# Six more key blocks on VectorE, feed-forward and output rows interleaved, and TensorE's waits divided, in a fused attention and gated feed-forward kernel

## The chip, the cores and the metric

One core of a Trainium2 chip runs the whole program. The metric is the device time of one execution in microseconds (us); the kernel before takes 685.96 us, the median of three runs from 685.57 to 686.65.

## The reference

The input x has 2048 rows of 512 values in bf16. Its layer norm xn feeds an attention with 32 heads of width 16 and a gated feed-forward of width 1792, and the result is the sum of both and x:

```python
xn = layernorm(x)                                  # 2048 x 512
q, k, v = split(xn @ wqkv)                         # 32 heads, 16 wide
p = softmax(q @ k.T * 16 ** -0.5)                  # per head, 2048 x 2048
A = merge(p @ v) @ wo
gate, up = xn @ W_gate, xn @ W_up                  # 2048 x 1792
B = (where(gate > 0, gate, 0) * up) @ W_down
out = x + A + B
```

The softmax has 32 x 2048 x 2048 exponentials, and these set the shape of the kernel.

## The kernel before, in words

**Tiling.** Queries come in four quarters of 512 (`c4`), heads in four groups of eight (`gg`), each in an even and an odd half (`ee`). That makes 32 *table blocks*, counted from 0 in the order of the work, and each of them goes over 16 *key blocks* of 128 keys for four heads.

**Two ways to exponentiate.** A key block on ScalarE is two *units*. A unit (loop at L1353) is two score groups on TensorE (`score`, L1289) into a PSUM buffer of two banks, of which there are two, and one exp over 128 x 1024 on ScalarE (L1365) into a ring of sixteen buffers. After both units come two groups that multiply with v (`pv_stream`, L1244). A key block on VectorE (`quad`, L1312) is four score groups, four evictions (L1320) that turn a score into an integer whose bits read as a bf16 exponential, two shifted copies of that (a *pattern* each), and six v groups, as the three approximations are summed. The string `QUAD_AT` (L67) says by table block and key block which key blocks go this way: a dot stays on ScalarE, and in the digit each bit says that one pattern is made on GpSimd, in two pieces (L1335), and otherwise on VectorE (L1339). With mask 2 the first pattern is VectorE's and the second GpSimd's. GpSimd's pieces wait by semaphore for VectorE's last pattern. 153 key blocks are on VectorE, and the other 359 are 718 units.

**TensorE's groups.** Nearly all matmuls are 64 x 32 tiles with 512 columns, issued as *groups* of four that fill one half of the array (64 rows); two groups, one in each half, run at the same time. Weights are loaded ahead in each half.

**Background jobs.** Projections of q, k and v, the feed-forward and the output rows run between the scores, through four further PSUM banks. A *feed-forward tile* (`glu`, L992) is two chains of eight groups, each with an eviction on VectorE (L1016, L1020), and gives an h tile of 128 x 512. An *output row tile* (`out_rows`, L1034) is 18 products, 36 groups: fourteen h tiles with `W_down` and four head groups with `wo`; one VectorE addition of x (L1069) and a store end it. `mm_chain` (L816) makes the groups. All of a row's groups name the same `reads`: all h tiles, all of `W_down`, `wo` and the attention results, so the first of them waits for all. After the feed-forward tiles of a quarter come its four output rows together (L1114); h has 20 slots. The rows of the last quarter come at the end and hold back part of their sum for a tail (`normalise_last`, L1136).

**What sets the order.** The program isn't scheduled when it is built: the string `PLAN` lists all operations in the order of a planner made beforehand, and the slots of their buffers (`run`, L324). Each engine takes its operations strictly in that order. `emit` (L380) turns dependencies into semaphores. `play` (L475) issues, before an operation, one wait per semaphore that it needs; where there are several, all but one become instructions of their own on the engine's queue (recorded at L483). DMAs go through SP's queue, and a stream of DMAs shares one semaphore.

Of the kernel before, what the change touches and what calls it, by code (L numbers as in the profile page):

```python
# [16 lines left out]
S = 2048  # L17
# [26 lines left out]
ROW_AT = 20  # L44
XBANKS = (0, 1, 2, 3)
# [32 lines left out]
    "2...3..3..2..3..",  # L78
    "2...3..3..0..3..",
    "2...3..3..2..3..",  # L80
# [5 lines left out]
    "3...3..3..2..3..",  # L86
    "2...2..3..0..3..",
    "2...3..3..2..3..",
    "2...3..3..2..3..",
# [4 lines left out]
    "2...3..3..2..3..",  # L94
    "2...3..3..0..3..",
    "2...3..3..2..3..",
# [145 lines left out]
class Op:  # L242
    __slots__ = ("eng", "dur", "fn", "deps", "order", "prio", "acq", "name", "idx", "start", "end",
                 "done", "left", "users", "signal", "sem", "val", "waits", "stream", "lat", "seq", "cseq", "hb", "after", "mode", "half", "bank", "urgent", "slack", "port",
                 "load", "wsrc", "wkey", "wwaits", "pair")


def matmul_loaded(e, out, w, x, start, stop, at):

    return e.add_instruction(mybir.InstMatmult(  # L250
        name=e.bass.get_next_instruction_name(), engine=mybir.EngineType.PE, ins=[e.lower_ap(x), e.lower_ap(w)], outs=[e.lower_ap(out)],
        start_tensor_calc=start, stop_tensor_calc=stop, tile_size=(64, 32), tile_position=at, ldweights=False))
# [1165 lines left out]
```

## Time and profile before

| | |
|---|---|
| median of the runs, us | 685.96 |
| the profiled execution: span from first to last instruction, us | 684.2 |
| its time outside the span | not given by the profile |
| granted TensorE clock, mean | 0.999 |
| exps on ScalarE (L1365) | 718 |
| score evictions on VectorE (L1320) | 612 |
| patterns on VectorE (L1339), pieces on GpSimd (L1335) | 83, 446 |
| 64 x 32 matmuls in the exp phase (10.9 to 674.2 us) | 21,959 |

Each engine's busy time is the union of its instructions. TensorE (PE), its weight loads (PEld) and ScalarE (ACT) overlap the end of one instruction with the next, so a short wait between two needn't show as idle time; starts in the timeline show it. A row of the timeline joins equal instructions without idle time between them: start, length, engine, line, operation and count, and in brackets the idle time before and what ended it. A row of the windows view has for each engine the busy time and the number of instructions in that window.

### The profile page before, as it was taken

Reading aid. Unit: us, or ns where it says so; the run is one execution under the profiler, and the core shown is the slowest. Engines: PE = TensorE matmul, PEld = TensorE weight load, DVE = VectorE, ACT = ScalarE, POOL = GpSimd, SP = SyncE. Lnnn points to the kernel's source line nnn. Section 1 sums busy time; section 2 is a strip of 40 time slices with the busy share of each in tenths; the row PEclk is TensorE's granted clock in tenths of the full one; section 3 lists DMA queues with packets and bytes.
Section 4 is the critical chain, followed back from the end, with each engine's and each line's share of the span. In section 5 each row is a group of like instructions: output and inputs, shape, how many; then the busy total and the mean of one; then the engine's idle time right before and its main releaser. Section 6 shows DMA issues by size and latency. Waiting matters only on the chain.

```text
span 684.2 us, 45020 instructions
## 1 busy us (share of the span) xinstructions
PE 675.6 (99%) x22262; PEld 345.9 (51%) x19654; DVE 598.5 (87%) x1012; ACT 666.8 (97%) x730; POOL 499.8 (73%) x507
## 2 busy tenths in 40 slices
PE   8999999999999999999999999999999999999998
PEld 4455454545555554554444455554554455555543
DVE  9958899999989787999999788889998887988875
ACT  6999999999999999999999999999999999999994
POOL 3323768678688778887587886888878868787792
PEclk9999999999999999999999999999999999999999
DMA  7430220113122021212101022120202012131011
GB/s 216 57 75 12 58 77 27 33 55 91 56 65 66 5 77 34 69 41 63 35 23 31 10 78 63 38 69 5 56 27 61 25 53 62 44 86 42 22 36 54
DMA packets 55940, 35.86 MB, mean 52 GB/s; under 512 B 19336, under 2 KB 51784, under 8 KB 55752
## 3 DMA queue, kind: packets, MB, share of 16 engines
q1 hardware_dynamic: 55464, 32.71, 17.4%
q8 instruction: 164, 2.69, 1.6%
q10 hardware_dynamic: 288, 0.26, 0.1%
q14 instruction: 24, 0.20, 0.1%
HBM read 26.35 MB, written 2.35 MB: 42 GB/s over the span
## 4 chain that ended last, share of the span: by engine, by line
PE 75%; ACT 18%; DVE 5%; issue 1%; DMA 0%; POOL 0%; ACTq 0%
PE ps L250 75%; ACT ring L1365 18%; DVE stats L726 1%; DVE qd L1320 1%; DVE xn_sb L739 1%; DVE v_aug L876 0%; DMA x_sb<-in_A_x_dram 0%; DVE qT L952 0%; DVE mv L727 0%; ACT xn_sb L1164 0%; DVE qd L1339 0%; DVE xnT L780 0%; POOL rstd L721 0%; DVE xnT L1075 0%; DVE kT L869 0%
## 5 line engine op out<-in xcount | busy, mean ns | idle before, releaser
L1365 ACT ACTIVATE ring<-ps 128x1024 bf16<-128x1024 f32 x718 | 660.4, 1141 | 2.9 <-PE ps L250 2.5
L1335 POOL TENSOR_TENSOR qd<-qd,ints 128x512 int32<-128x512 int32 x446 | 450.5, 1041 | 143.8 <-DVE qd L1339 73.2
L250 PE MATMUL ps<-qT,kT 64*32 64x512 bf16 x8192 | 448.7, 374 | 1.3 <-DVE qd L1320 0.4
L1320 DVE TENSOR_SCALAR qd<-ps 128x512 int16<-128x512 f32 x612 | 396.7, 685 | 51.9 <-PE ps L250 49.0
L250 PE MATMUL ps<-qd,v_aug 64*32 64x512 bf16 x3672 | 263.0, 375 | 1.1 <-issue 0.9
L250 PE MATMUL ps<-ring,v_aug 64*32 64x512 bf16 x2872 | 236.5, 374 | 0.1
L1300 PEld LDWEIGHTS <-kT 64*32 64x32 bf16 x7584 | 151.1, 92 | 126.6 <-issue 32.6
L1272 PEld LDWEIGHTS <-v_aug 64*32 64x32 bf16 x4544 | 108.7, 91 | 75.6 <-issue 20.4
L250 PE MATMUL ps<-xnT,wgs 64*32 64x512 bf16 x1792 | 137.6, 374 | 0.0
L250 PE MATMUL ps<-xnT,wus 64*32 64x512 bf16 x1792 | 136.4, 374 | 0.0
L250 PE MATMUL ps<-Wd,hT 64*32 64x512 bf16 x768 | 59.0, 375 | 0.0
L810 PEld LDWEIGHTS <-wgs 64*32 64x32 bf16 x1792 | 43.1, 91 | 31.5 <-issue 7.4
L810 PEld LDWEIGHTS <-wus 64*32 64x32 bf16 x1792 | 43.2, 91 | 29.8 <-issue 7.6
L1339 DVE TENSOR_SCALAR qd<-qd 128x2048 int16<-128x2048 int16 x83 | 56.1, 690 | 2.3 <-PE ps L250 2.2
L810 PEld LDWEIGHTS <-hT 64*32 64x32 bf16 x1792 | 40.2, 92 | 28.2 <-issue 4.2
L250 PE MATMUL ps<-Wv,hT 64*32 64x512 bf16 x512 | 45.7, 375 | 0.0
L250 PE MATMUL ps<-Wk,hT 64*32 64x512 bf16 x512 | 42.8, 375 | 0.4 <-DVE qd L1320 0.3
L1020 DVE SCALAR_TENSOR_TENSOR hT<-ps,up_sb 128x512 bf16<-128x512 f32 x56 | 38.4, 685 | 4.6 <-PE ps L250 4.2
L1016 DVE COPY up_sb<-ps 128x512 f32<-128x512 f32 x56 | 38.4, 685 | 3.1 <-PE ps L250 2.5
L250 PE MATMUL ps<-Wo_p,x_sb 64*32 64x512 bf16 x480 | 40.2, 374 | 0.6 <-issue 0.5
L250 PE MATMUL ps<-xnT,Wq 64*32 64x512 bf16 x480 | 36.2, 375 | 0.0
L250 PE MATMUL ps<-xnT,Wk 64*32 64x512 bf16 x480 | 35.0, 374 | 0.3 <-DVE xnT L780 0.3
(70 smaller groups left out, 263.8 us busy)
## 6 DMA issues: line engine op xcount, KB each, us to landing
rb<-rec_scr SPq DMA_DIRECT2D x31, 256.0 KB
wus<-in_B_W_up_dram SPq DMA_DIRECT2D x38, 128.0 KB, 2.8
wgs<-in_B_W_gate_dram SPq DMA_DIRECT2D x38, 128.0 KB, 3.3
xr_sb<-in_A_x_dram SPq DMA_DIRECT2D x16, 128.0 KB, 2.6
qT<-qf SPq DMA_DIRECT2D x120, 16.0 KB, 2.6
out_dram<-xn_sb SPq DMA_DIRECT2D x14, 128.0 KB, 2.0
x_sb<-in_A_x_dram SPq DMA_DIRECT2D x8, 128.0 KB, 2.8
x_sb<-oT SPq DMA_DIRECT2D x60, 16.0 KB, 2.5
```

The costliest lines, as they stand in the source:

```text
L250: return e.add_instruction(mybir.InstMatmult(name=e.bass.get_next_instruction_name(), engine=mybir.EngineType.PE, ins=[e.lower_ap(x), e.lo ...
L726: G.op("DVE", 580, lambda e, m=m: e.bn_stats(stats[:, m, :], xs(m)), reads=[t_xm[m]], writes=[t_st], prio=pr, order=last_xn if m == 4 else ())
L739: G.op("DVE", 320, lambda e, m=m, t=t_n: e.tensor_scalar(xn_sb[:, t.slot, :], xs(m), mv[:, m, 0:1], rstd[:, m:m + 1], op0=ALU.subtract, op ...
L810: e.ldweights(w()[rows, 32 * j:32 * j + 32], tile_position=(rows.start, 32 * j))
L1016: G.op("DVE", 603, lambda e: e.tensor_copy(up_sb[:, tup.slot, :], bank_of(tu)), reads=[tu], writes=[tup], prio=-590)
L1020: G.op("DVE", 603, lambda e: e.scalar_tensor_tensor(out=hT[:, th.slot, :], in0=bank_of(tg), scalar=0.0, in1=up_sb[:, tup.slot, :], op0=ALU ...
L1272: e.ldweights(vs(j), tile_position=(64 * half, 32 * j))
L1300: e.ldweights(ks(m), tile_position=(64 * half, 32 * m))
L1320: G.op("DVE", 601, lambda e, j=j, tx=tx: e.tensor_scalar(qd[:, tq.slot, 512 * j:512 * j + 512], ps[:, BANK[tx.slot], :], IBIAS[3], 0.0, op ...
L1335: G.op("POOL", POOL_NS / POOL_PIECES + 60, lambda e, x=x, n=n, c=slice(i * m, i * m + m): e.tensor_tensor(x().bitcast(I32)[:, c], raw().bi ...
L1339: G.op("DVE", 600, lambda e, n=n, x=x: e.tensor_scalar(x(), raw(), float(SHIFTS[n + 1]), None, op0=ALU.add), reads=[ti, tq], writes=[t], p ...
L1365: exp_ops[u] = G.op("ACT", 904, lambda e, tr=tr, k0=k0: e.activation(ring[:, tr.slot, :, :], ps[:, 4 * k0:4 * k0 + 2, :], ACTF.Exp, scale= ...
```

## The change

Four things change together, and the order of the plan with them: `PLAN_OPS` goes from 8248 to 8302, and `PLAN` is another string (left out here).

1. Six strings of `QUAD_AT`, those of table blocks 10, 12, 18, 21, 26 and 28, get a sixth key block on VectorE, all with mask 2. It is 159 key blocks on VectorE then, and 706 units.
2. The output rows of a quarter are held back (`behind`) and dealt out between the feed-forward tiles of the next quarter, one after each `ROW_STEP` of them: none, one, two and two. As the h tiles live longer for that, twelve more h slots lie in `xnT`, in the quarters whose projections are done (`h_of`, and the guards at the end).
3. With `each=True`, a product in an output row reads only its own h tile and its own slice of the weights (`only`), so its groups wait part by part.
4. In `emit`, where a TensorE operation has several waits, all but the latest are moved, where possible, to one of the eight operations before it: to its second to fourth matmul, at most three. The producer must stand more than 20 places of the plan before that carrier, or 70 if it is a DMA.

Besides, the packing DMAs of attention results use four semaphores each in place of two.

```diff
+ROW_STEP = (0, 1, 2, 2)
...
-    "2...3..3..2..3..",
+    "2.2.3..3..2..3..",
...
-    "3...3..3..2..3..",
+    "3.2.3..3..2..3..",
...
+CARRIED = []
 def matmul_loaded(e, out, w, x, start, stop, at):
+    if at[1] and CARRIED:
+        e.wait_ge(*CARRIED.pop(0))
...
+    CARRY_BACK, CARRY_AGE, CARRY_AGE_DMA = 8, 20, 70
...
+        for i, o in enumerate(q):
+            best = {}
+            for d in o.waits:
+                s, v = d.sem
+                if id(s) not in best or best[id(s)][1] < v:
+                    best[id(s)] = (s, v, d)
+            for s, v, d in sorted(best.values(), key=lambda b: b[2].start)[:-1]:
+                for p in q[max(0, i - self.CARRY_BACK):i][::-1]:
+                    if p.mode != "half" or p.start <= d.start + (self.CARRY_AGE_DMA if d.eng == "SP" else self.CARRY_AGE):
+                        break
+                    if len(carried.get(p, ())) < 3:
+                        carried.setdefault(p, []).append((s, v))
+                        moved_off.setdefault(o, set()).add(id(s))
+                        break
...
-                wait(o.waits)
+                wait(o.waits, moved_off.get(o, ()))
+                CARRIED[:] = carried.get(o, ())
...
-        P_h = Pool("h", NHS)
+        P_h = Pool("h", NHS + 12)
...
-                    G.op("PE", 216, fn, reads=reads, joins=[tile],
+                    need = reads[i] if each else reads
+                    G.op("PE", 216, fn, reads=need, joins=[tile],
...
+        def h_of(t):
+            if t.slot < NHS:
+                return hT[:, t.slot, :]
+            a, dt = divmod(t.slot - NHS, 4)
+            return xnT[:, dt, 512 * a:512 * a + 512]
...
-            th = t_h[(c4, ft)] = Tile("h", P_h)
+            th = t_h[(c4, ft)] = Tile("h", P_h, list(range(NHS)) + [NHS + 4 * a + dt for a in range(c4) for dt in range(4)
+                                                               if c4 < NB - 1 or a == 2 or dt in TAIL_ACT])
...
-            pairs, reads = [], [t_wo]
+            pairs, reads = [], []
             if first:
-                reads += [t_h[(c4, ft)] for ft in range(FT)] + [t_wd]
                 for ft in range(FT):
+                    reads.append([t_h[(c4, ft)], only(t_wd, ft)])
...
-                reads.append(to)
+                reads.append([to, only(t_wo, g)])
...
-            mm_chain(t, pairs, reads, pr, slots=slots, sub=sub)
+            mm_chain(t, pairs, reads, pr, slots=slots, sub=sub, each=True)
...
-            seq += rows
+            step = ROW_STEP[c4]
+            for n, row in enumerate(behind):
+                seq += tiles[n * step:n * step + step] + [row]
+            seq += tiles[len(behind) * step:]
+            behind = rows
+        seq += behind
...
-                    stream=("pk", j, (n // 2) % 2), name="pk")
+                    stream=("pk", j, (n // 2) % NGG), name="pk")
...
+        for a in range(3):
+            guard = Tile("xnT")
+            guard.r.extend(o for o in t_xnT[a].w + t_xnT[a].r if o not in resids)
+            P_h.cur[NHS + 4 * a:NHS + 4 * a + 4] = [guard] * 4
```

More of the change, by code (lines that the diff above doesn't have):

```diff
@@ L367, in run @@
                 port[o.eng] = o
-            o.seq = len(self.queue[o.eng])
+            o.seq, o.start = len(self.queue[o.eng]), i
             self.queue[o.eng].append(o)
@@ L814, in bass_parallel_sum__mha_block__glu_gated_reglu__prompt_kernel, with mm_chain @@
         chains = [0]
-        def mm_chain(tile, pairs, reads, prio, sub=0, slots=None, mode="half", weights=None, flags=None):
+        def mm_chain(tile, pairs, reads, prio, sub=0, slots=None, mode="half", weights=None, flags=None, each=False):
             n = len(pairs)
@@ L1032, in resid, with only @@
             return xnT[:, i, 0:1024].bitcast(FP32)
+        def only(t, n):
+            part = Tile()
+            part.w.append(t.w[n])
+            return part
         def out_rows(c4, i, gs, first, last, slots=None, pr=0.0, tile=None, sub=0):
```

234 lines of the change are left out of this document (122 added, 112 removed).

## The prediction

> **What bounds the kernel now.** First the page's totals, the chain, and the costliest groups.
>
> ```profile
> span 684.2 us, 45020 instructions
> ...
> PE 675.6 (99%) x22262; PEld 345.9 (51%) x19654; DVE 598.5 (87%) x1012; ACT 666.8 (97%) x730; POOL 499.8 (73%) x507
> ...
> PE 75%; ACT 18%; DVE 5%; issue 1%; DMA 0%; POOL 0%; ACTq 0%
> ...
> L1365 ACT ACTIVATE ring<-ps 128x1024 bf16<-128x1024 f32 x718 | 660.4, 1141 | 2.9 <-PE ps L250 2.5
> L1335 POOL TENSOR_TENSOR qd<-qd,ints 128x512 int32<-128x512 int32 x446 | 450.5, 1041 | 143.8 <-DVE qd L1339 73.2
> L250 PE MATMUL ps<-qT,kT 64*32 64x512 bf16 x8192 | 448.7, 374 | 1.3 <-DVE qd L1320 0.4
> L1320 DVE TENSOR_SCALAR qd<-ps 128x512 int16<-128x512 f32 x612 | 396.7, 685 | 51.9 <-PE ps L250 49.0
> ...
> L1339 DVE TENSOR_SCALAR qd<-qd 128x2048 int16<-128x2048 int16 x83 | 56.1, 690 | 2.3 <-PE ps L250 2.2
> ```
>
> TensorE at 99% and ScalarE at 97% cannot both be believed: both pipeline, so busy time hides short waits. The starts decide. Two answers of the timeline of ScalarE alone: the whole run, then a stretch without a wait.
>
> ```profile
> 10.91 2.87 ACT L1365 ACTIVATE ring<-ps 128x1024 bf16<-128x1024 f32 x3
> 14.10 146.19 ACT L1365 ACTIVATE ring<-ps 128x1024 bf16<-128x1024 f32 x159 [0.32 <-PE ps L250]
> 160.47 2.85 ACT L1365 ACTIVATE ring<-ps 128x1024 bf16<-128x1024 f32 x3 [0.17 <-PE ps L250]
> 163.63 22.10 ACT L1365 ACTIVATE ring<-ps 128x1024 bf16<-128x1024 f32 x24 [0.31 <-PE ps L250]
> 186.10 38.83 ACT L1365 ACTIVATE ring<-ps 128x1024 bf16<-128x1024 f32 x42 [0.37 <-PE ps L250]
> 225.36 182.36 ACT L1365 ACTIVATE ring<-ps 128x1024 bf16<-128x1024 f32 x198 [0.42 <-PE ps L250]
> 408.64 265.61 ACT L1365 ACTIVATE ring<-ps 128x1024 bf16<-128x1024 f32 x289 [0.92 <-PE ps L250]
> 680.25 0.60 ACT L1164 ACTIVATE xn_sb<-ps 128x512 bf16<-128x512 f32 x1 [6.00 <-PE ps L250]
> ```
>
> ```profile
> 126.28 19.35 ACT L1365 ACTIVATE ring<-ps 128x1024 bf16<-128x1024 f32 x21
> ...
> 144.36 2.19 ACT L1365 ACTIVATE ring<-ps 128x1024 bf16<-128x1024 f32 x2
> ```
>
> From the first exp of that stretch to the 21st are 20 intervals in 144.36 - 126.28 = 18.08 us: **0.904 us** from exp to exp when nothing is late, although one exp lasts 1.14 us. The exps run from 10.91 to 408.64 + 265.61 = 674.25 us, 663.3 us. 717 intervals at 0.904 us are 648.2, the last exp adds 1.1, and 14.0 us are left: **lateness**, 20 ns per exp. Every visible one of these waits ends on a TensorE score. Before the first exp stand 10.9 us, after the last 10.0 us. So ScalarE sets the pace for 98% of the exp phase, and TensorE's lateness for the other 2%.
>
> TensorE has room in spite of its 99%:
>
> ```profile
> 10.90:674.20 663.30, 659.61 (x21959) 338.40 (x19374) 585.20 (x969) 660.39 (x719) 493.62 (x492) 1.00 0.18 50
> ```
>
> ```profile
> 407.72 0.39 PE L250 MATMUL ps<-qd,v_aug 64*32 64x512 bf16 x4
> 407.74 0.38 PE L250 MATMUL ps<-Wd,hT 64*32 64x512 bf16 x4
> ...
> 407.94 0.39 PE L250 MATMUL ps<-qd,v_aug 64*32 64x512 bf16 x4
> ...
> 407.96 0.38 PE L250 MATMUL ps<-Wd,hT 64*32 64x512 bf16 x4
> ```
>
> Eight matmuls, four in each half of the array, start every 0.21 to 0.22 us. The exp phase has 21,959 of them: 2,745 such rounds, at 0.215 us 590 us of 663, or 89%. The full clock is granted (1.00).
>
> **The change, part by part.** *Six more blocks on VectorE.* A key block on ScalarE is two exps; one on VectorE is four evictions (L1320), one pattern on VectorE (L1339), two pieces on GpSimd (L1335; all six have mask 2), ten groups of four matmuls in place of six. Twelve exps go: 12 x 0.904 = **10.85 us** off the binding engine. The cost goes beside it:
> - TensorE: 6 x 4 groups more, 96 matmuls, 12 rounds x 0.215 = 2.6 us, in the 73 us that rounds leave free now (about 60 are left).
> - GpSimd: 12 pieces x 1.04 = 12.5 us, in 184 us of idle time.
> - VectorE: 6 x 5 instructions. Back to back they take less than their 0.685 us:
>
> ```profile
> 222.16 2.48 DVE L1320 TENSOR_SCALAR qd<-ps 128x512 int16<-128x512 f32 x4 [0.26 <-PE ps L250]
> ```
>
> (2.48 - 0.685)/3 = 0.60 us, so 30 x 0.60 = 18.0 us, in 684.2 - 598.5 = 85.7 us of idle time. Over the whole run all three fit. Locally it is narrow:
>
> ```profile
> 268.94:288.92 19.98, 19.98 (x688) 9.74 (x596) 18.58 (x31) 19.98 (x24) 17.59 (x18) 1.00 0.21 59
> 390.14:411.39 21.25, 20.35 (x724) 12.00 (x628) 16.92 (x28) 20.34 (x24) 18.59 (x19) 1.00 0.25 71
> ```
>
> These windows are table blocks 12 and 18, both of which get a sixth block on VectorE. Block 12 shrinks to 20 x 0.904 = 18.1 us, and VectorE has 18.6 us there now; with 3.0 more it would have 21.6. It fits only if 3.5 us go elsewhere. That is what the second part does.
>
> *Jobs moved.* Feed-forward tiles cost VectorE two evictions per 16 matmul groups, output rows one per 36. Block 18, with output rows, leaves VectorE 4.3 us free, block 12, with feed-forward tiles, 1.4. Dealing the rows out between the next quarter's tiles mixes the two. No job is added or dropped, and the row loads keep their number on SP's queue; the packing DMAs get four semaphores in place of two, which only takes a wait away. The twelve extra h slots lie in spent quarters of xnT, and their writers wait for readers of a quarter before. I count the move at nothing by itself: it hides the 18 us. If that cover fails, the price is that of the one block with six now, below.
>
> *Rows part by part.* The first row's first group waits now for all fourteen h tiles and all weights together. Views of the queues' own waits and of the weight loads at the first row:
>
> ```profile
> L483 PEldq EVENT_SEMAPHORE  x130: 51/51/407, 6.6 to 673.4; - x130
> ```
>
> ```profile
> 224.21 0.12 PEld L810 LDWEIGHTS <-hT 64*32 64x32 bf16 x4 [0.73 <-DVE qd L1320]
> ```
>
> TensorE stops 0.73 us there, and the next exp is late by much of it (225.36, idle 0.42). Output rows start four times. Between nothing and 4 x 0.73 = 2.9 us goes; I take 0.9, one such stop and a small second.
>
> *Waits spread.* 130 wait instructions of 51 ns are 6.6 us of TensorE's queue. TensorE is 11% free, so between nothing and 6.6 us comes back; I take nothing. A carried wait sits on a matmul up to eight groups (8 x 0.11 = 0.9 us) ahead of its user, and behind it queue the next scores, and behind those ScalarE. It is carried only if the producer was placed over 20 plan positions earlier (70 for a DMA): 8,248 positions in 663 us are 0.08 us each, so 1.6 and 5.6 us. The larger losses have another cause, as the 0.92 us before 408.64, where TensorE stood still with no producer:
>
> ```profile
> 407.51 0.39 PE L250 MATMUL ps<-qd,v_aug 64*32 64x512 bf16 x4 [0.90 <-issue]
> ```
>
> Nothing in the change addresses that.
>
> *What the sixth block costs.* One table block has six already, block 6; its 20 exps and the 22 of the next, from the timeline in windows:
>
> ```profile
> 147.14 13.16 ACT L1365 ACTIVATE ring<-ps 128x1024 bf16<-128x1024 f32 x14
> ...
> 166.36 19.38 ACT L1365 ACTIVATE ring<-ps 128x1024 bf16<-128x1024 f32 x21
> ...
> 187.03 19.58 ACT L1365 ACTIVATE ring<-ps 128x1024 bf16<-128x1024 f32 x21
> ```
>
> Block 6 took 166.36 - 147.14 = 19.22 us, 1.14 over 20 x 0.904; at the run's 20 ns per exp it would be 0.39 over. Surplus 0.75 us. The next, with five, was 20.67 - 19.89 = 0.78 over, so block 6 is not far out. Between 0 and 0.75 per new block, 0 to 4.5 in all; I take a third, 1.5, since the move spreads VectorE's load.
>
> *Sum.* 684.2 - 10.85 - 0.9 + 1.5 = 673.95 us of span. The profile gives no time of its own beyond the span; the median shown, 685.96, is 1.8 above it, and I keep that: **675.7 us**.
>
> A rule speaks against the six patterns. A pattern can meet a piece on GpSimd:
>
> ```profile
> 541.30 2.04 POOL L1335 TENSOR_TENSOR qd<-qd,ints 128x512 int32<-128x512 int32 x2 [1.13 <-DVE qd L1339]
> ```
>
> ```profile
> 542.91 0.97 DVE L1339 TENSOR_SCALAR qd<-qd 128x2048 int16<-128x2048 int16 x1
> 544.44 0.69 DVE L1320 TENSOR_SCALAR qd<-ps 128x512 int16<-128x512 f32 x1 [0.56 <-PE ps L250]
> ```
>
> The pattern started 0.43 us before the piece ended and took 0.97 us in place of 0.69. The Trainium skill, SBUF — State Buffer, section Who interferes with whom, says that VectorE in a two-port mode and GpSimd lock each other out of a shared port for a whole instruction. The trace agrees in kind, with 0.28 us lost. What it would do here is the third rival.
>
> **The rivals.**
> 1. *Levelling pays more.* The holes before the rows and part of the 6.6 us of waits go, and the sixth block costs nothing: -2.9 and -2 in place of +0.6 give 670.2. For it: the row stop is visible. Against: the waits are short and TensorE is not full.
> 2. *The new blocks run like block 6.* +4.5 in place of +1.5: 678.7, or 679.7 with none of the 0.9. For it: block 12's account.
> 3. *Pattern and pieces exclude each other.* If each new pattern waits out one 1.04 us piece and the scores come late by as much: 6 x 1.04 = 6.2 us, 675.7 + 6.2 = 682. Against: ScalarE shows no idle time after 542.91 until 674.25, and GpSimd and patterns together are 499.8 + 56.1 of 684.2 us.
> 4. *TensorE is the bound* and its free 11% cannot be used, as the chain's 75% may be read: then the exps saved give nothing, and 12 rounds cost 2.6 x 663/590 = 2.9 us: 688.9. Against: the unbroken 0.904 us.
> 5. *Slower: VectorE falls behind from block 10 on* and never catches up, so that all later exps come as late as in block 6, 57 ns each. From 225.36 on there are 487 exps, late by 8.4 us now (448.9 - 486 x 0.904 - 1.1). Some 475 at 57 ns are 27.1: 675.7 + 18.7 = 694. It decides from the point where those exps are late by 8.4 + 10.85 us, 40 ns each. For it: in the exp phase VectorE goes from 585.2 of 663.3 us (88%) to 603 of 652 (92%), and more in feed-forward stretches. Against: 49.0 us of its own waits are for TensorE.
> 6. *A carried wait blocks scores,* so the change does not do what it says: eleven stops of 1 us eat the gain, about 686. For it: a producer later than planned by over 0.7 us is enough.
>
> **How the numbers follow.** Forecast 0.60 (672 to 679), levelling 0.10, block 6's pace 0.09, port 0.04, TensorE bound 0.04, VectorE behind 0.09, blocked waits 0.04. The forecast's own bounds are 684.2 - 10.85 + 1.8 = 675.2, less 2.9 and plus 4.5. The runs shown differ by 0.16%, so 0.2% (1.4 us) is about what can be told from no change. Faster: 0.60 + 0.10 + 0.09 + 0.04 = 0.83; within: 0.04; slower: 0.13. The range from 669.5 to 683 leaves out the last three (0.17) and a little of rival 1.
>
> **What would show it.** ScalarE: 706 exps, the unbroken spacing still 0.904 us, first exp near 10.9, the last end near 664, lateness 12 to 17 us. VectorE: 636 x L1320 and 89 x L1339, busy 610 to 620 us. GpSimd: 458 pieces. Fewer than 130 wait instructions on TensorE, and no stop of 0.7 us at the first row. It is wrong if lateness exceeds 25 us, if exps in blocks 10 to 31 average over 40 ns late, or if the spacing itself changes.

## The result, and the profile after

The change makes the kernel slower: 697.25 us (median of four runs, 696.78 to 697.48) against 686.06 us for the kernel before on the same chip (four runs, 685.57 to 686.65). The ratio is 1.0162, with a 95% interval of 1.0149 to 1.0174. 675.7 was forecast, in a range up to 683.

The page of the kernel after: totals, the chain that ended last, and the groups that answer to those shown of before. Lines have moved: L1418 is the exp (L1365 before), L263 the matmul (L250), L1373 the eviction (L1320), L1392 the pattern (L1339), L1388 the GpSimd piece (L1335).

```profile
span 695.6 us, 46326 instructions
...
PE 689.4 (99%) x22358; PEld 390.2 (56%) x20914; DVE 620.0 (89%) x1042; ACT 671.5 (97%) x718; POOL 511.9 (74%) x519
...
PE 95%; DVE 4%; POOL 1%; DMA 0%; ACT 0%; issue 0%; ACTq 0%
```

The shares of busy time have hardly moved, and say nothing: TensorE (PE) has 99% in both kernels. The chain has moved. ScalarE (ACT) held 18% of it before and holds nothing now; the chain runs along TensorE for 95% of the span. The groups of TensorE by form, first of before and then of after, show it from another side (count, busy union in us, mean ns):

```profile
L250 PE MATMUL ps<-qT,kT 64*32 64x512 bf16 x8192 | 448.7, 374 | 1.3 <-DVE qd L1320 0.4 <-DVE xnT L1075 0.2
L250 PE MATMUL ps<-qd,v_aug 64*32 64x512 bf16 x3672 | 263.0, 375 | 1.1 <-issue 0.9
```

```profile
L263 PE MATMUL ps<-qT,kT 64*32 64x512 bf16 x8192 | 502.9, 375 | 0.7 <-issue 0.3 <-ACT ring L1418 0.2
L263 PE MATMUL ps<-qd,v_aug 64*32 64x512 bf16 x3816 | 300.6, 375 | 0.4 <-POOL qd L1388 0.3
```

The score matmuls are 8,192 in both, each 0.375 us long, but the time that they cover together grows from 448.7 to 502.9 us: fewer of them run side by side. ScalarE's timeline has become a string of short pieces:

```profile
10.91 2.87 ACT L1418 ACTIVATE ring<-ps 128x1024 bf16<-128x1024 f32 x3
14.10 32.57 ACT L1418 ACTIVATE ring<-ps 128x1024 bf16<-128x1024 f32 x35 [0.32 <-PE ps L263]
46.95 80.15 ACT L1418 ACTIVATE ring<-ps 128x1024 bf16<-128x1024 f32 x85 [0.28 <-PE ps L263]
127.44 24.55 ACT L1418 ACTIVATE ring<-ps 128x1024 bf16<-128x1024 f32 x26 [0.34 <-PE ps L263]
...
394.95 5.72 ACT L1418 ACTIVATE ring<-ps 128x1024 bf16<-128x1024 f32 x6 [0.49 <-PE ps L263]
401.24 18.13 ACT L1418 ACTIVATE ring<-ps 128x1024 bf16<-128x1024 f32 x19 [0.56 <-PE ps L263]
...
603.77 81.85 ACT L1418 ACTIVATE ring<-ps 128x1024 bf16<-128x1024 f32 x87 [0.35 <-PE ps L263]
```

The second row has 35 exps in 32.57 us, 0.93 us each and not 0.904: most lateness shows no gap. The exps now run from 10.91 to 603.77 + 81.85 = 685.62 us. Of these 674.7 us, 705 intervals at 0.904 are 637.3 and the last exp adds 1.0: **lateness is 36.4 us**, against 14.0 before. So 10.85 us of exps went, as forecast, and 22.4 us of lateness came; that is, but for rounding, the 11.4 us by which the span grew, 684.2 to 695.6.

**Where it came from.** Table blocks 1 to 8 come ahead of the first new block (block 10). One answer of the windows view of each kernel, from the first exp of block 1 to that of block 9:

```profile
core 0: us, PE busy (x) PEld busy (x) DVE busy (x) ACT busy (x) POOL busy (x), PEclk, DMA share, GB/s
41.00:207.40 166.40, 165.89 (x5556) 87.03 (x4948) 149.50 (x243) 165.50 (x182) 112.44 (x111) 1.00 0.20 55
```

```profile
41.00:213.90 172.90, 172.18 (x5580) 98.28 (x5328) 151.74 (x246) 170.15 (x182) 110.86 (x110) 1.00 0.20 56
```

The work is the same but for 24 matmuls and three instructions of VectorE (DVE), and the stretch takes 172.90 us in place of 166.40. So 6.5 us of the 22.4 arise where nothing was added. The moved rows aren't there yet either: in both kernels the first output row loads its weights, the h tiles, only after this stretch (first and last start, in us, behind the colon):

```profile
L810 PEld LDWEIGHTS <-hT x1792: 88/92/93, 224.2 to 680.6; 64*32 64x32 bf16 x200
```

```profile
L842 PEld LDWEIGHTS <-hT x1440: 88/93/94, 224.8 to 692.1; 64*32 64x32 bf16 x180
```

What differs there is the new `PLAN`, which interleaves the groups of the same jobs in another way, orders the other engines' queues anew and deals out other buffers, and the carried waits, which the first experiment takes away. The new order loads weights more often (5,328 loads in place of 4,948). Over the whole program, 917 groups wait by semaphore for a group of the other half in the same PSUM bank, where 754 did. The lateness by table block, from the first exp of each block in both traces, says the same: blocks 1 to 8 gain 0.8 us each, blocks 10 to 31 0.7 us each. The six blocks with a sixth key block are late by 5.3 us together, in place of 2.3: 0.5 us more each. The other 26 bear the remaining 19.4 us.

### The profile page after: what moved, and what is told of

Its sections match the earlier page's. It is cut to its first block, busy times and chain, and to the rows that moved or that the text cites. A ratio compares the mean times of both kernels' runs of the same rounds, so it can differ in the third digit from the quotient of the medians.

```text
span 695.6 us, 46326 instructions
## 1 busy us (share of the span) xinstructions
PE 689.4 (99%) x22358; PEld 390.2 (56%) x20914; DVE 620.0 (89%) x1042; ACT 671.5 (97%) x718; POOL 511.9 (74%) x519
## 4 chain that ended last, share of the span: by engine, by line
PE 95%; DVE 4%; POOL 1%; DMA 0%; ACT 0%; issue 0%; ACTq 0%
PE ps L263 95%; DVE stats L758 1%; DVE v_aug L909 1%; DVE xn_sb L771 0%; POOL qd L1388 0%; DVE qd L1373 0%; DMA x_sb<-in_A_x_dram 0%; DVE qT L985 0%; DVE mv L759 0%; POOL x_sb L1280 0%; ACT xn_sb L1217 0%; DVE xnT L812 0%; POOL rstd L753 0%; DVE kT L902 0%; DVE kT L999 0%
## 5 line engine op out<-in xcount | busy, mean ns | idle before, releaser
L1418 ACT ACTIVATE ring<-ps 128x1024 bf16<-128x1024 f32 x706 | 665.0, 1034 | 9.7 <-PE ps L263 5.8
L1388 POOL TENSOR_TENSOR qd<-qd,ints 128x512 int32<-128x512 int32 x458 | 462.2, 1039 | 147.9 <-DVE qd L1392 101.5
L263 PE MATMUL ps<-qT,kT 64*32 64x512 bf16 x8192 | 502.9, 375 | 0.7 <-issue 0.3
L1373 DVE TENSOR_SCALAR qd<-ps 128x512 int16<-128x512 f32 x636 | 416.1, 685 | 44.2 <-PE ps L263 40.1
L263 PE MATMUL ps<-qd,v_aug 64*32 64x512 bf16 x3816 | 300.6, 375 | 0.4 <-POOL qd L1388 0.3
L263 PE MATMUL ps<-ring,v_aug 64*32 64x512 bf16 x2824 | 242.9, 375 | 0.0
L1353 PEld LDWEIGHTS <-kT 64*32 64x32 bf16 x7912 | 171.1, 92 | 106.2 <-issue 13.3
L1325 PEld LDWEIGHTS <-v_aug 64*32 64x32 bf16 x5476 | 131.7, 92 | 77.5 <-issue 7.0
L263 PE MATMUL ps<-xnT,wgs 64*32 64x512 bf16 x1792 | 144.6, 375 | 0.0
L263 PE MATMUL ps<-xnT,wus 64*32 64x512 bf16 x1792 | 139.8, 375 | 0.0
L1392 DVE TENSOR_SCALAR qd<-qd 128x2048 int16<-128x2048 int16 x89 | 61.3, 695 | 0.3
L263 PE MATMUL ps<-Wd,hT 64*32 64x512 bf16 x608 | 54.6, 375 | 0.0
L263 PE MATMUL ps<-Wo_p,x_sb 64*32 64x512 bf16 x480 | 43.0, 375 | 0.0
L263 PE MATMUL ps<-Wv,hT 64*32 64x512 bf16 x448 | 41.3, 375 | 0.0
L263 PE MATMUL ps<-xnT,Wq 64*32 64x512 bf16 x480 | 36.6, 374 | 0.0
L263 PE MATMUL ps<-Wv,xnT 64*32 64x512 bf16 x576 | 36.3, 374 | 0.1
L263 PE MATMUL ps<-xnT,Wk 64*32 64x512 bf16 x480 | 35.6, 374 | 0.5 <-DVE xnT L812 0.3
L263 PE MATMUL ps<-Wk,hT 64*32 64x512 bf16 x384 | 35.2, 375 | 0.0
```

The costliest lines, as they stand in the source:

```text
L263: return e.add_instruction(mybir.InstMatmult(name=e.bass.get_next_instruction_name(), engine=mybir.EngineType.PE, ins=[e.lower_ap(x), e.lo ...
L1325: e.ldweights(vs(j), tile_position=(64 * half, 32 * j))
L1353: e.ldweights(ks(m), tile_position=(64 * half, 32 * m))
L1373: G.op("DVE", 601, lambda e, j=j, tx=tx: e.tensor_scalar(qd[:, tq.slot, 512 * j:512 * j + 512], ps[:, BANK[tx.slot], :], IBIAS[3], 0.0, op ...
L1388: G.op("POOL", POOL_NS / POOL_PIECES + 60, lambda e, x=x, n=n, c=slice(i * m, i * m + m): e.tensor_tensor(x().bitcast(I32)[:, c], raw().bi ...
L1392: G.op("DVE", 600, lambda e, n=n, x=x: e.tensor_scalar(x(), raw(), float(SHIFTS[n + 1]), None, op0=ALU.add), reads=[ti, tq], writes=[t], p ...
```

## The experiments

All runs below were timed in rounds with the kernel before on the same chip, which took 686.9 to 688.7 us there. "Ratio" is to that kernel, with its 95% interval. The kernel after wasn't timed again in these rounds; where one of its variants is set against 697.25 us, the comparison is of times from different rounds, and by the ratios it can come out up to 0.4% otherwise.

### Carried waits, and the parts that cost nothing

```diff
-    CARRY_BACK, CARRY_AGE, CARRY_AGE_DMA = 8, 20, 70
+    CARRY_BACK, CARRY_AGE, CARRY_AGE_DMA = 0, 20, 70
```

> The changed kernel with nothing carried: every extra wait of TensorE is its own instruction again, all else the same. Theory O (the new plan's order of TensorE's groups leaves one half of the array idle in too many rounds): 696 to 699 us, within 2 us of the change's 697.25, with 100 to 135 wait instructions. Theory C (carried waits stop TensorE inside a group and hold back the scores behind it): at least 5 us less, 692 or below. Theory V (VectorE falls behind): no difference, 696 to 699.

Measured 697.29 us, ratio 1.012 (1.0098 to 1.0141), where after had 697.25 and 1.0162. By the times the carried waits cost nothing, by the ratios 0.4% at most: they aren't the cause of the 1.6%, and blocks 1 to 8 are late by 9.7 us without them and by 10.2 with them (3.7 in before). The other way round, before with parts 3 and 4 of the change and four packing semaphores, but its own plan and 153 blocks:

> The kernel before, with its own plan and its 153 blocks, and only two parts of the change: output rows wait part by part (with the four packing semaphores that this needs), and waits are carried. Theory O: 683 to 687 us, as the order of TensorE's groups is that of before; at best 2 us gained at the first rows. Theory C: 690 or more. Theory V: 683 to 687.

Measured 685.72 us against 688.44, ratio 0.996 (0.9937 to 0.9984): these parts gain 0.4%. The wait instructions on TensorE's queue are 63 in after, in place of 130, and the row's stop is gone as well. The view of the waits' line in after, and the weight loads of the h tiles in before and in after (where 352 more read the h slots in `xnT` and are counted there):

```profile
L514 PEldq EVENT_SEMAPHORE  x63: 51/51/51, 6.9 to 683.4; - x63
```

```profile
L810 PEld LDWEIGHTS <-hT 64*32 64x32 bf16 x1792 | 40.2, 92 | 28.2 <-issue 4.2 <-DVE qd L1320 2.2
```

```profile
L842 PEld LDWEIGHTS <-hT 64*32 64x32 bf16 x1440 | 35.0, 92 | 23.5 <-issue 2.2
```

The 2.2 us of waiting for VectorE have gone.

### Is ScalarE the pace? Exps of 768 columns

```diff
-    lambda e, ...: e.activation(ring[:, tr.slot, :, :], ps[:, 4 * k0:4 * k0 + 2, :], ...
+    lambda e, ..., c=slice(0, 512 if u < 64 else 384): e.activation(ring[:, tr.slot, :, c], ps[:, 4 * k0:4 * k0 + 2, c], ...
```

> The changed kernel with shorter exps: from unit 64 on each exp takes 768 of the 1024 columns, so the rest of its ring buffer keeps older values; ScalarE is no longer near the bound. Theory O: TensorE's order sets the pace, so the time stays within 4 us of 697 (693 to 698). Theory V: VectorE sets the pace and it stays too (693 to 698), but the idle time of VectorE in front of its evictions stays small. If ScalarE were the bound, 642 units at about 0.2 us less would take far over 50 us away.

> The kernel before with the same shorter exps (768 of 1024 columns from unit 64 on, older values in the rest). This measures how near TensorE's own pace stood to ScalarE's before the change. If my prediction was right about the kernel before (ScalarE the bound, TensorE with 11% of room that can be used), it falls by 40 us or more, to 645 or less. Theory O: TensorE's order allows little more than ScalarE does already, 676 to 684 us, and the kernel before stays at least 10 us below the changed one with the same exps.

After: 697.38 us, ratio 1.0125 (1.01 to 1.0151), unchanged. Before: 684.18 us, ratio 0.9931 (0.9909 to 0.9953), though ScalarE lost 76 us of work. The page of before with short exps:

```profile
PE 673.1 (98%) x22259; PEld 362.7 (53%) x19654; DVE 597.8 (87%) x1012; ACT 590.9 (86%) x730; POOL 499.2 (73%) x507
...
PE 91%; DVE 6%; DMA 2%; issue 1%; ACT 0%; POOL 0%; SPq 0%; ACTq 0%; DVEq 0%
```

The reading that ScalarE alone set the pace of before falls here: with ScalarE out of the chain, TensorE's chain was nearly as long.

### Is it TensorE's products? Lighter feed-forward

```diff
-                (lambda dt=dt: xnT[:, dt, 512 * c4:512 * c4 + 512])
+                (lambda dt=dt: xnT[:, dt, 512 * c4:512 * c4 + 256])
```

The same line changes for the up and for the gate products, and each matmul writes as many columns as it reads.

> The kernel after with the up and gate products of the feed-forward part computed for half of the rows only (256 of 512 columns): 896 of TensorE's 5,560 groups are half as long, 96 us of work of a half array or 48 us of rounds, with the order, the waits and all other engines as they are. Theory O or any theory with TensorE as the bound: 10 to 30 us off, 667 to 687. Theory V: within 3 us of 697.

> The kernel before with the up and gate products of the feed-forward part computed for half of the rows only, as above. If TensorE's queue paced the kernel before as well: 6 to 14 us off (14 us is all its lateness), 672 to 680. The prediction's reading (ScalarE paces, TensorE has 73 us of room): 0 to 3 us off. With the exps a quarter shorter it had gained only 0.7% (684.18).

After: 686.47 us, ratio 0.9993 (0.9979 to 1.0007), 10.8 us off. Before: 687.27 us, ratio 0.9997 (0.9981 to 1.0013), nothing. The chains, of before and then of after with the light products:

```profile
ACT 54%; PE 39%; DVE 5%; DMA 1%; issue 1%; POOL 0%; SPq 0%; ACTq 0%; DVEq 0%
```

```profile
PE 68%; ACT 24%; DVE 6%; POOL 1%; issue 0%; DMA 0%; ACTq 0%; DVEq 0%; POOLq 0%
```

In after, shorter matmuls bring the time down, and ScalarE back into the chain. In before they only hand the chain to ScalarE. If before is held by both side by side, both reliefs at once must pay more than their sum:

> The kernel before with both reliefs at once: exps of 768 instead of 1,024 columns from unit 64 on (alone: 684.18, 0.7% off), and the up and gate products for half of the rows (alone: 687.27, no change). Theory K (before is held by ScalarE's exps and by TensorE's queue side by side, so that relief of one leaves the other): 8 to 16 us off, 670 to 679. If a third engine holds before, or the order of the queues whatever the durations: 681 to 687.

Measured 675.51 us, ratio 0.9804 (0.9787 to 0.9822): 13.2 us, where the two alone gave 4.3 and 0.2. **Before is held by ScalarE and TensorE at once.** The page of this kernel still has TensorE at 98%:

```profile
span 673.6 us, 45020 instructions
...
PE 659.8 (98%) x22262; PEld 367.1 (54%) x19654; DVE 596.2 (89%) x1012; ACT 585.2 (87%) x730; POOL 499.2 (74%) x507
...
PE 76%; DVE 12%; ACT 8%; DMA 1%; issue 1%; POOL 0%; SPq 0%; ACTq 0%; DVEq 0%
```

### Is it the number of TensorE's instructions?

After has 1,260 weight loads more than before. More instructions in before, as loads done twice or as matmuls split in two:

```diff
-            elif held[o.half] == o.wkey:
+            elif held[o.half] == o.wkey and (again := again + 1) % 2:
```

> The kernel before, which loads weights anew in half of the 652 places where it had left a load out because the half of the array holds these weights already: 326 groups of four loads, 1,304 more instructions in TensorE's queue (after has 1,260 more loads than before), with the order of the groups, their waits and their products as they are. Theory I (TensorE's queue is paced by its number of instructions, matmuls and loads alike, at about 15 ns each in the densest stretches of 16 us and more): 8 to 14 us slower, 694 to 701. Theory L (each weight load holds up its half of the array, whatever the number of instructions): the same. Theory O (the order of the groups alone): 0 to 3 us, 686 to 690, since the loads lie beside matmuls.

> The kernel before, in which 336 groups of the up products (those that neither begin nor end a sum) are issued as eight matmuls of 256 columns instead of four of 512: 1,344 more instructions, the same number of columns, no more weight loads, the same order. Theory I: 6 to 14 us slower, 692 to 701. Theory L and theory O: 0 to 3 us, 686 to 690.

691.07 us, ratio 1.0069 (1.0048 to 1.0089), and 692.13 us, ratio 1.007 (1.0037 to 1.0102): about 5 us either way. Some 1,300 instructions cost that much in before's order, loads and matmuls alike; the 8 to 14 us expected were too much for the loads, and the 6 to 14 for the matmuls were hardly reached. Fewer loads, where the groups concerned carry the key "bare":

```diff
-            elif held[o.half] == o.wkey:
+            elif held[o.half] == o.wkey or o.wkey == "bare":
                 o.load, o.wsrc = False, ()
```

> The kernel after without the weight loads of 336 groups of the up products (they are computed with whatever weights the half of the array holds): with those that then fall out by themselves 1,476 loads fewer, 41,749 instructions of TensorE instead of 43,219 (before has 41,930); order, waits and matmuls as they are. Theories I and L: back to about the time of before, 683 to 690. Theory O: 694 to 698.

> The kernel after without the weight loads of all 896 groups of the up and gate products (computed with whatever weights the array holds): 3,900 loads fewer, 39,336 instructions of TensorE. Theories I and L: the queue gets some 58 us of its 15 ns places back, and the exps are the pace again: 706 by 0.904 behind the first 10.9 us, and 11 us at the end, are 660; so 665 to 680. Theory O: 692 to 698.

> The kernel before without the weight loads of all 896 groups of the up and gate products (computed with whatever weights the array holds): 3,968 loads fewer, in the old order. Theory T: before's order leaves few stalls, and the instructions are its nearer limit; 3 to 8 us off, 678 to 684. If instructions aren't a limit of before: within 2 us, 684 to 688.

After without 1,476 and 3,900 loads: 697.01 us, ratio 1.0155 (1.014 to 1.017), and 697.06 us, ratio 1.0152 (1.0137 to 1.0167). Before without 3,968: 685.64 us, ratio 0.9983 (0.9969 to 0.9997). The theory that the instructions hold after falls, and before gained 1.3 us where theory T expected 3 to 8. The page of after with 3,900 loads fewer:

```profile
PE 688.2 (99%) x22355; PEld 337.2 (49%) x17014; DVE 620.5 (89%) x1042; ACT 671.1 (97%) x718; POOL 511.9 (74%) x519
```

Weight loads are down from 390.2 us to 337.2, and the span from 695.6 to 695.0.

### Does another order of TensorE's queue help?

The order of the plan is kept on four engines, and on TensorE replaced by one that was worked out from the durations in the records so that the halves wait less for each other:

```diff
+        d = zlib.decompress(base64.b85decode(ORDER))
+        self.queue["PE"] = [self.queue["PE"][i + d[i] - 128] for i in range(len(d))]
```

> The kernel after with another order of TensorE's own queue and nothing else: 4,678 of its 5,597 places hold another group than in the plan (by 2 places in the middle, at most 40), with the same groups, the same queues of the other four engines, the same PSUM places, and no waits carried on earlier matmuls (that alone changed nothing: 697.29). Theory O (TensorE's strictly ordered queue sets the time, and the new plan's order of groups is the costly part): at least 8 us off, 675 to 688. Theory V (VectorE, with 18 us more work, no longer keeps up, or PSUM comes free too late): within 3 us of 697, since VectorE's work and order are untouched. If TensorE is bound by the mere number of its groups: within 3 us of 697 too.

> The kernel before with another order of TensorE's own queue and nothing else: 4,363 of 5,573 places hold another group (by 2 places in the middle, at most 38). Theory O: before was paced by that order as well, though less; 675 to 682, so 4 to 11 us off. The prediction's reading (ScalarE's 718 exps set the pace, only 14 us of lateness in all, TensorE has room): at most the 14 us of lateness could go, and the likeliest is 0 to 3 us, since a late exp would be late again on the next thing.

Neither gain came: 698.03 us, ratio 1.016 (1.0124 to 1.0196), and 697.46 us, ratio 1.015 (1.0119 to 1.0182). The first lies where theory V put it, within 3 us of 697; the second lies outside every forecast. These orders load weights more often (21,384 and 20,556 loads), so both limits were lifted together, and then two orders with fewer loads than these were tried:

> The kernel after with both edits that changed nothing alone: the other order of TensorE's queue (698.03 alone), and the up and gate products without their weight loads, computed with whatever weights the array holds (697.06 alone); no carried waits. Theory T (two limits on one queue: the order of the groups with its waits, and some 15 ns for each instruction; the other order lifts the first but brings more instructions into each stretch, leaving out loads lifts the second alone): now both are lifted, 680 to 688. Theory S (the time of after is set elsewhere, by VectorE or by the PSUM places, since neither edit moved it): 695 to 698.

> The kernel after with an order of TensorE's queue that was chosen for both limits: few waits of one half on the other, and fewer weight loads than after (20,372 instead of 20,796); 4,517 of 5,597 places hold another group, by at most 38 places; all else as in after, with its carried waits. Theory T: 680 to 690, 7 to 17 us off. Theory S: 695 to 699.

> The kernel before with the carried waits, the rows that wait part by part and the two more packing semaphores (685.72 without more), and an order of TensorE's queue that was chosen for both limits (4,100 of 5,573 places hold another group; 19,840 loads instead of 19,536). Theory T: 677 to 684. If before's order was already as good as the two limits allow: 684 to 688. With the first other order, which had 1,020 more loads, it was 697.46.

697.39 us, ratio 1.0155 (1.0129 to 1.0181); 695.61 us, ratio 1.014 (1.0124 to 1.0155); 690.91 us, ratio 1.0063 (1.0048 to 1.0078). Theory T falls; theory S, that VectorE or the PSUM places set the time of after, fits its two runs. One line of the page of before in the other order (b_order):

```profile
PE 70%; ACT 26%; DMA 2%; DVE 1%; issue 1%; SPq 0%; POOL 0%; ACTq 0%; DVEq 0%
```

ScalarE's share of the chain grew from 18% to 26% and the span by 10.7 us. What these experiments show is that the same groups in another order of one queue move before by 10 us (687.43 to 697.46), of which its 1,020 further loads would be some 3 at the rate of b_loads. They do not show which order would be good.

They also narrow down what makes the new plan costly. Matched with the program's order, the records have 297 groups in after, and 170 in before, that start within 0.455 us of a group of the other half whose bank they take over. In a_order they are 186 and in a_best2 218, and the time is about the same; blocks 1 to 8 are late by 9.1 us in a_order and by 7.9 in a_best2, still far from the 3.7 of before. So the order of TensorE's own queue isn't shown to be what costs: all the other orders of after kept the new plan's queues of the other four engines and its PSUM places, and no run changes those.

### VectorE

```diff
-                    qd[:, tq.slot, 512 * j:512 * j + 512], ps[:, BANK[tx.slot], :], IBIAS[3], ...
+                    qd[:, tq.slot, 512 * j:512 * j + n], ps[:, BANK[tx.slot], :n], IBIAS[3], ...    # n = 512 if u < 100 else 256
```

> The kernel after with the table blocks' evictions on VectorE cut to 256 of 512 columns from unit 100 on (the rest of each raw tile keeps old values): some 550 evictions of 0.60 us become about half as long, 150 us less work for VectorE, with the order and everything else as it is. Theory V (VectorE alone holds after): 20 us off or more, 665 to 677. Theory J (after is held by TensorE's queue, with VectorE's evictions as links in the same chain, as the records of after give it: about half of the chain in steps of one half of the array, three tenths in round trips over VectorE, a tenth in waits of one half for the other's bank): 5 to 12 us off, 685 to 692. TensorE's rounds alone: 0 to 3 us, 694 to 698.

Measured 691.04 us, ratio 1.0035 (1.0022 to 1.0048) where after has 1.0162: about 1.3%, or 6 to 9 us. The page:

```profile
PE 683.4 (99%) x22358; PEld 380.1 (55%) x20914; DVE 492.6 (71%) x1042; ACT 667.7 (97%) x718; POOL 512.3 (74%) x519
...
PE 94%; DVE 4%; POOL 1%; DMA 0%; issue 0%; ACT 0%; ACTq 0%
...
L1373 DVE TENSOR_SCALAR qd<-ps 128x256 int16<-128x256 f32 (+1 forms) x636 | 274.6, 441 | 137.3 <-PE ps L263 126.9
```

VectorE is rid of 127 us of work and now waits 126.9 us for TensorE at its evictions, but the time falls by less than a tenth of that. VectorE doesn't hold after alone; its evictions are links in TensorE's chain.

The profile's chain can't show such links well: it steps back along TensorE's queue, and doesn't know the halves. So the records were also followed back with the program's own dependencies, from the last exp to 12 us: each operation to the one that released it last, where a group follows the one before it in its half, a group of the other half in its bank, or another engine. Microseconds of the chain, with the number of steps for the first two:

```
                          before          after          a_light        a_dve
next group in its half    300.6 (1346)    372.6 (1725)   269.5 (1253)   420.6 (1942)
other half's bank          33.6 (73)       71.3 (156)     44.4 (98)      84.3 (185)
to, on and from VectorE   187.4           205.5          224.4           79.7
to, on and from ScalarE   134.5            11.1          107.9           74.4
```

The split is rough: where two releases fall close together, it depends on the time that is allowed for the way from one engine to the next. With allowances from -60 to 120 ns, VectorE's share of before comes out as 105 to 141 us and ScalarE's as 202 to 233. What holds with all of them is the step from before to after: the waits for the other half's bank go from 19 to 28 us to 62 to 68, and ScalarE's share falls to 15 to 58.

Theory J was read from the column of after, and the time of a_dve bears it out: one chain that runs through the steps of a half, the waits between the halves, and VectorE.

## Why the prediction was wrong

**"TensorE has room": the failing step.** The forecast set 12 more rounds, 2.6 us, against 73 us of TensorE that it called free, and so put TensorE's cost at nothing. A share of rounds counts the array, not a queue whose groups follow one another within a half and also wait for evictions and for the other half. In the terms of the sum: 0.6 us of lateness net were forecast (-0.9 + 1.5), and 22.4 came. b_short and b_short_light show that already in before TensorE's chain was about as long as ScalarE's: easing ScalarE alone gave 0.7%, both 2.0%. The unbroken 0.904 us, on which the pace was based and which was held against rival 4, says that the scores came in time, not how early. The Trainium skill, Perfetto Trace Analysis, section Identifying the Most-Contended Engine, warns that busy time misjudges TensorE and names the weight loads' busy share as one of two better measures. The first half agrees (99% in before and after, 98% in the kernel that took 675.51 us); the second doesn't follow the time here, as the loads' share fell from 56% to 49% in a_fewer2 with 697.06 us in place of 697.25.

**"Jobs moved, counted at nothing": the second failure.** The reason given was that jobs were neither added nor dropped and that VectorE's load is evened out. VectorE did not fall behind: at its evictions it still waits 40.1 us for TensorE, where it waited 49.0.

```profile
DVE qd L1373 <- PE ps L263: 40.1, 102, 0.9
```

But the move, like the six blocks, came with a new plan of the whole program, and the forecast has no term for that. In blocks 1 to 8, where neither has begun, the plan costs 6.5 us at equal work, from the two windows; b_order shows that an order of one queue can cost some 7 us beside its further loads. That the new plan is what costs after the rest is argued from these and from the even lateness of all blocks, and not shown by itself: the six blocks and the move were not run apart, because each needs a plan of its own. Nor is it shown which part of the plan costs, as other orders of TensorE's queue left the time of after as it was.

**Exps.** Right in number (706), and so is the 10.85 us. The spacing without lateness is still 0.904 us, but only 240 of 705 intervals are at most 0.906 us, where 483 of 717 were. The 10.85 us could only be cashed where ScalarE is the pace.

**The sixth block.** 1.5 us forecast, bounds 0 to 4.5; the six blocks became 3.0 us later, 0.5 us each and less than the others on average.

**VectorE and GpSimd.** 18.0 and 12.5 us more forecast; 620.0 - 598.5 = 21.5 and 511.9 - 499.8 = 12.1 measured. Both fit, as said.

**Rows part by part, waits spread.** -0.9 and nothing forecast; together with the packing semaphores 688.44 - 685.72 = 2.7 us off, within the bounds. The 0.73 us that the forecast calls a stop of TensorE is the idle time of its weight loads; its matmuls stood idle for 0.28 us there (L250 at 224.25). The carried waits alone: 697.29 against 697.25, nothing, as forecast. Rival 6 falls with that.

**The rivals.** Rivals 1 and 2 only price the forecast's own terms otherwise, and miss with it. Rival 4 had the mechanism, TensorE as the bound with a free 11% that can't be used, and the wrong price: it charged only the 12 added rounds, 2.9 us, and no new order. Rival 5's 694 lies nearer, but its mechanism isn't borne out: lateness began in block 1, not 10, and a fifth of VectorE's work less (620.0 to 492.6 us) moved the time by 6 to 9 us. Rival 3, the port, wasn't tried by itself, but the patterns themselves hardly changed: 695 ns on average in place of 690, over 89 of them. Both marks set for failure were passed: lateness is 36.4 us, over 25, and the exps of blocks 10 to 31 are late by 50 ns on average, over 40.

**What stays open.** Which part of the new plan costs: the order of TensorE's queue, that of the other engines' or the PSUM places; why the orders tried did no better; and how much of the 22.4 us the six blocks would cost in a plan as good as before's.

## What to carry to other kernels

An engine's idle or free share need not be room where its queue is in order: before something is moved beside the pace-maker, ease the pace-maker in an experiment, and see whether the time follows; if it doesn't, a second engine stands right behind. When a change brings a new order of the whole program, compare stretches that do the same work in both: what differs there is the new order's and the new buffers'. And price the new plan: a change that adds little work can cost more by it than all that it saves.

## What the hardware showed that was not expected

More weight loads cost time and fewer gave little back: 1,304 more in before cost 4.2 us, some 3 ns each, and 1,344 more matmuls with the same columns as much (5.2 us), but 3,968 loads fewer in before gained only 1.3 us, and 3,900 fewer in after nothing (697.06 in place of 697.25 us). More loads weren't tried in after.

A group that takes over a PSUM bank from the other half starts at the earliest some 0.44 us after that group's start (0.445 us is the commonest distance in the records of after), about two of the 0.215 us steps in its own half. The wait is the program's own. The Trainium skill, PSUM — Partial Sum Buffer, section PSUM bank collisions raise a hardware error, gives its reason, that different row tiles can't use one bank at the same time and software has to keep them apart; no run here tries it without.

Where no wait holds them, the halves don't keep the queue's order between them: of after's 5,560 groups, 1,035 start over 0.03 us before the group just ahead of them in the queue, which belongs to the other half.
